# Mamba-2 scan and switch routing: one last routing group of eight units, two experts limited after 16 units, and the first job read and turned like the others

## The chip, the cores and the metric

The kernel runs on one core of a Trainium2 chip. The metric is the device time of one execution in microseconds (us). Of nine runs of the kernel before, the median is 258.06 us, the lowest 257.04 and the highest 258.99.

## The reference, cut to what matters

Two blocks follow each other. The first is a state-space scan: for 4 batches, 8 heads and 768 positions, each head keeps a 16 x 32 state that fades with `a`, and the output is `C` times the state. The reference does it in chunks; the kernel takes chunks of 128 positions, with the same result. The second block sends each of the 3072 tokens (256 wide) to one of eight experts, the one with the largest logit, and multiplies what the expert gives by the softmax weight of that expert.

```python
M = einsum('bhin,bhjn->bhij', Cc, Bc) * L          # masked, decayed scores
y[:, :, sl] = einsum('bhij,bhjd->bhid', M, xc) + y_inter
state = decay_full * state + sum(Bx, axis=2)
...
x = y.transpose(0, 2, 1, 3).reshape(N, 256)
logits = x @ w_gate
expert_idx = argmax(logits, axis=1)
for e in range(8):
    mask = expert_idx == e
    out[mask] = gate_w[mask, None] * (maximum(x[mask] @ w1[e], 0) @ w2[e])
```

## The kernel before

**Units and steps.** A unit is one batch and one chunk of 128 positions, all eight heads: 24 units. A step `d` takes two units, 2d and 2d + 1, and there are 12 steps (`ND`), written out in an order made by hand (L756 to L848; no planner moves instructions, each engine runs its own in the order in which they are emitted). In a step:

- `scores` (L270) multiplies C by B on TensorE; it is emitted at the end of the step before. `weigh` (L276) masks the result on VectorE into the tile M.
- `y_old` (L315) adds what the carried state gives, `y_own` (L325) what the chunk itself gives, both into the PSUM tile `y_ps`.
- `own` (L282) makes the chunk's own part of the new state, in columns 256 to 383 of the first bank of `y_ps` (`A_ps`). `state` (L301) takes it out on ScalarE, `faded` and `whole` add the old state. In the last two steps there is none of this.
- `turned` (L333) copies `y_ps` to the SBUF tile yT on ScalarE. One step later `rows(k)`, k = d - 1 (L341), multiplies yT by a constant on TensorE, which gives token rows and their partial logits in the PSUM tile `r_ps`. `rows_out` (L347) scales them into a row tile on VectorE, and `logits_of` (L364) sums the logits.

**Routing.** Units are routed in groups (`RGS`, L27), six of four units. When a group's rows are there, `choose` (L369) and `count` (L404) find each token's expert and count them; one step later `rank` (L379, TensorE) and `ranked` (L395, VectorE) give each token its place in the DRAM tensor `x_hbm`, in which each expert has an area of its own. `place` (L417) sends a unit's 128 rows there with an indirect DMA of GpSimd; these wait in a list `todo`. An expert's first 256 rows are its first job, the rest its second. So that a first job can be loaded before all tokens are routed, `cut` (L425) raises the expert's count to at least 256 after a group: later tokens then go to the second job. Expert 0 is limited after 16 units (step 9), expert 1 after 20 (step 11). Rows of a first job that no token got were emptied at the start.

**Jobs.** After the loop, the scan's tiles are given back (`att.close()`, L849), and PSUM is divided anew: four banks `h_ps` and two `y_ps` (L539). Jobs 0 to 7 are the experts' first 256 rows. `m_load` (L468) reads a job's rows from `x_hbm`, on the DMA queue of SyncE (SP), behind the places of all rows written before it. For jobs from 1 on it reads them as xb, in four DMAs, such that VectorE's 32 x 32 block transpose (`m_xT`, L521) gives the transposed xT, and once more the rows' ends as lt. Job 0 reads whole rows (tile xs, one DMA), and `m_xT0` (L511) turns them with four TensorE transposes and two ScalarE copies. `gates` (L494) works out the softmax weight on VectorE with one exponential on ScalarE. `m_h` (L560) makes the up products, eight blocks f of 128, with a relu each on ScalarE; `between(f)` (L868) hangs other work between the blocks. `m_y` (L587) makes the down products, `put` (L574) scales them and sends them out with an indirect DMA of GpSimd. The second jobs go in pairs (L619), with a size chosen at run time from the counts: 128 to 192 rows in steps of four.

After the loop, the order before is: the places still in `todo` (units 16 to 19), four weight loads, `m_load(1)`, then rows, rows_out and logits of step 11, `m_xT0`, `choose` and `count` of the last group (units 20 to 23), `gates` of job 0, and the jobs. The last group's rank, its four places and the loads of jobs 2 and 3, with eight weight loads between them, hang behind block 1 of job 0. `over` (L436), behind block 4 of job 1, checks the counts and finds the pairs' sizes.

Of the kernel before, what the change touches and what calls it, by code (L numbers as in the profile page):

```python
# [13 lines left out]
ALU = mybir.AluOpType  # L14
# [11 lines left out]
AMIN = 0.75  # L26
RGS = [4, 4, 4, 4, 4, 4]  # L27
CUT = 4
# [19 lines left out]
def ssd_then_moe(ctx, tc, xs_in, ae_in, wgx, w_gate, w1, w2, gx, gb, gc, ga, out):  # L48
# [232 lines left out]

    def own(d):  # L282
        if d // NP == NC - 1:
            return
        for s in range(2):
            for q in range(4):
                nc.tensor.matmul(A_ps[32 * q:32 * q + 32, 64 * s:64 * s + 64],
                                 lhsT=st[2 * d + s]["B"][:, 32 * q:32 * q + 32],
                                 rhs=st[2 * d + s]["xp"][:, 64 * q:64 * q + 64], start=(s == 0), stop=True,
                                 skip_group_check=True)  # L290
# [41 lines left out]

    def turned(d, a=0, b=KT):  # L333
        if a == 0:
            sd[d]["yT"] = wk.tile([128, KT, 2 * CH], FP32, name="yT")
        nc.scalar.copy(out=sd[d]["yT"][:, a:b], in_=y_ps[:, a:b, 0:2 * CH])  # L336

    rt = [(sm if i < CUT else sm2).tile([128, n, W], FP32, name=f"rows{i}") for i, n in enumerate(RGS)]
    grp = [g for g, n in enumerate(RGS) for _ in range(n)]

    def rows(d):  # L341
        for t, s in [(t, s) for t in range(KT) for s in range(2)]:
            nc.tensor.matmul(r_ps[:, s, 256 * t:256 * t + 160], lhsT=sd[d]["yT"][:, t, CH * s:CH * s + CH],  # L343
                                 rhs=turn[:, t].rearrange("p e h -> p (e h)"), start=True, stop=True,
                                 skip_group_check=True)

    def rows_out(d):  # L347
        n = 2 * d
        g = grp[n]
        k = n - R0[g]  # L350
        for a, b, o in ((0, D, 0), (D, DE, DM)):
            nc.vector.tensor_tensor(
                out=rt[g][:, k:k + 2, o:o + KT * 4 * (b - a)].rearrange("p s (t e h) -> p s t e h", t=KT, h=4),
                in0=r_ps.rearrange("p s (t z) -> p s t z", t=KT)[:, :, :, 4 * a:4 * b].rearrange(
                    "p s t (e h) -> p s t e h", h=4),
                in1=bc(Er[:, n:n + 2].rearrange("p s (t h) -> p s t h", h=4)[:, :, :, None, :],
                       [128, 2, KT, b - a, 4]), op=ALU.mult)
# [62 lines left out]
    def counts(g):  # L420
        p = r_ps[:, 1, 460:460 + E]
        nc.tensor.matmul(p, lhsT=ones_bf, rhs=cnt[:, g], start=True, stop=True, skip_group_check=True)
        return p

    def cut(e):  # L425


        p = r_ps[:, 1, 460:460 + E]
        c = cnt[0:1, CUT + e, e:e + 1]
        nc.vector.tensor_scalar(out=less[:, e:e + 1], in0=p[0:1, e:e + 1], scalar1=-float(P1), scalar2=0.0, op0=ALU.add,  # L430
                                op1=ALU.min)
        nc.vector.tensor_tensor(out=c, in0=c, in1=less[:, e:e + 1], op=ALU.subtract)
        if e == 0:
            nc.vector.tensor_reduce(bad[:, 0:1], p[0:1, 0:2], axis=AX, op=ALU.min)

    def over():  # L436
        p = r_ps[:, 1, 460:460 + E + 1]
        nc.tensor.matmul(p[:, 0:E], lhsT=ones_bf, rhs=cnt[:, len(RGS)], start=True, stop=True, skip_group_check=True)
# [29 lines left out]
    def m_load(i):  # L468


        p, e = jobs[i]
        if i == 0:
            xs = mo.tile([128, 2, W], FP32, name="xs")
            nc.sync.dma_start(out=xs, in_=x_hbm[e * NR:e * NR + P1, :].rearrange("(t p) w -> p t w", p=128))
            ex[i]["xs"] = xs
            ex[i]["lt"] = xs[:, :, DM:W]
            return
        r0, n = e * NR + P1 * p, (P1, P2)[p]
        xb = mo.tile([128, P1 // 32 * 64], FP32, name="xb", bufs=4)
        for c in range(4):  # L480
            nc.sync.dma_start(out=xb[32 * c:32 * c + 32, 0:2 * n].rearrange("p (r z) -> p r z", z=64),
                              in_=x_hbm[r0:r0 + n, 64 * c:64 * c + 64].rearrange("(r j) z -> j r z", j=32))
        ex[i]["xb"] = xb[:, 0:2 * n].rearrange("p (r i k) -> p k r i", k=KT, i=32)
        lt = mo.tile([128, 2, MID], FP32, name="lt", bufs=7)[:, 0:2 - p]
        nc.sync.dma_start(out=lt, in_=x_hbm[r0:r0 + 128 * (2 - p), DM:W].rearrange("(t p) w -> p t w", p=128))
        ex[i]["lt"] = lt
        if p and e % 2 == 0:
            lh = mo.tile([128, 1, MID], FP32, name="lh", bufs=3)
            for u in range(2):
                q = r0 + u * NR + 128  # L490
                nc.sync.dma_start(out=lh[64 * u:64 * u + 64, 0], in_=x_hbm[q:q + 64, DM:W])
            ex[i]["lh"] = ex[i + 1]["lh"] = lh
# [17 lines left out]

    def m_xT0():  # L511

        ex[0]["xT"] = mo.tile([128, KT, P1], FP32, name="xT", bufs=4)
        for k in range(KT):
            q = h_next()[:, 0:P1]
            for t in range(2):
                xs = ex[0]["xs"][:, t, 0:DM].rearrange("p (i k) -> p i k", k=KT)
                nc.tensor.transpose(q[:, 128 * t:128 * t + 128], xs[:, :, k], ident)
            nc.scalar.copy(ex[0]["xT"][:, k], q)  # L519

    def m_xT(i):  # L521
        p, e = jobs[i]
        n = (P1, P2)[p]
        for j in range(i, i + 1 + p):
            ex[j]["xT"] = mo.tile([128, KT, P1], FP32, name="xT", bufs=4)
            nc.vector.transpose(ex[j]["xT"][:, :, 0:n].rearrange("p k (r j) -> p k r j", j=32), ex[j]["xb"])  # L526
        for j in range(i, i + 1 + p):
            ex[j]["g"] = gates(ex[j]["lt"], 2 - p)
        if p:
            ex[i]["gh"] = gates(ex[i]["lh"], 1)  # L530

    H, Y, turn_no = [], [], [0, 0]
    hT_all = [mo.tile([128, FT, P1], FP32, name=f"hT{k}") for k in range(3)]
# [5 lines left out]
    def psum(pp):  # L539
        for k in range(4):  # L540
            H.append(pp.tile([128, 512], FP32, name=f"h_ps{k}"))
        for k in range(2):
            Y.append(pp.tile([128, 512], FP32, name=f"y_ps{k}"))

# [173 lines left out]
    with tc.manual_schedule():  # L718
# [37 lines left out]
        for d in range(ND):  # L756
# [23 lines left out]
            if k >= 0:  # L780
                rows(k)
            own(d)
            if d == 0 or d == 4:
# [4 lines left out]
            q = late.get(d)  # L788
            e_cut = {9: 0, 11: 1}.get(d)
            if q is not None:  # L790
                rank(q)
                if e_cut is not None:
                    counts(CUT + e_cut)
            weigh(2 * d)
            weigh(2 * d + 1)
            if d == 0:
                take_totals(0)
                inverse(0, p0, 4, 12)
            if d < ND - 1:
                for s in range(2):  # L800
                    y_own(d, s, range(NH))
                if d == 4:
                    turn_both(1)
                turned(d)
                if d == 4:
                    take_both(1)
            else:
                for t in range(KT):
                    for s in range(2):
                        y_own(d, s, range(4 * t, 4 * t + 4))  # L810
                for t in range(KT):
                    turned(d, t, t + 1)
            state(d)
# [3 lines left out]
            if q is not None:  # L817
                ranked(q)
                if e_cut is not None:
                    cut(e_cut)  # L820
                todo += list(range(R0[q], R0[q] + RGS[q]))
            if k >= 0:
                rows_out(k)
                if d == 4:
                    take_totals(1)
            if d == 0:
                route_consts()
            if k >= 0:
                logits_of(k)
# [15 lines left out]
            if d == 10:  # L845
                m_load(0)
            if d == 11:
                weakest()  # L848
        att.close()  # L849
        w2pool = ctx.enter_context(tc.tile_pool(name="w2pool", bufs=1, reuse_waits="tile"))  # L850
        pp = ctx.enter_context(tc.tile_pool(name="pp", bufs=1, space=PSUM, reuse_waits="tile"))
        psum(pp)
        for e in range(EW, E):
            w_sb.append([w2pool.tile([128, KT * F], FP32, name=f"w{u + 1}_{e}") for u in range(2)])
        while todo:
            place(todo.pop(0))
        for k in range(4):
            load_w(1, 1, k)
        m_load(1)
        rows(ND - 1)  # L860
        rows_out(ND - 1)
        logits_of(ND - 1)
        m_xT0()
        choose(LAST)
        count(LAST)
        ex[0]["g"] = gates(ex[0]["lt"], 2)
        for i in range(E):
            def between(f):  # L868
                if i == 0:
                    if f == 1:  # L870
                        rank(LAST)
# [3 lines left out]
                        m_load(2)  # L875
                        for k in range(8):
                            load_w(2, *divmod(k, 4))
                        m_load(3)
# [104 lines left out]
```

## Time and profile before

| | |
|---|---|
| median of 9 runs | 258.06 us |
| the profiled execution | 257.07 us |
| its span, first to last instruction | 255.3 us |
| mean granted TensorE clock | 0.983 |
| busy: TensorE | 242.0 us (95%) |
| busy: VectorE, ScalarE, GpSimd | 88.3, 88.9, 84.4 us (33 to 35%) |
| up products of the experts (L557) | 512 matmuls, 91.1 us |
| down products (L592) | 384 matmuls, 85.1 us |
| DMA | 39.75 MB, mean 156 GB/s |

The timeline has one row for instructions of one form that follow each other on an engine: start and length in us, engine, line, operation, tiles, shapes, count, and in brackets the idle time before it and what ended that. "PE" is TensorE, "DVE" VectorE, "ACT" ScalarE, "POOL" GpSimd, "SPq" the DMA issues of SyncE. In the table of windows a row has the stretch, its length, the busy time and count of each engine, the granted TensorE clock as a share, the DMA share and GB/s. L12 is line 12 of the kernel before. A wait's releaser is inferred from semaphore events; ends of matmuls are modelled.

### The profile page before, as it was taken

The numbers are of one execution on the slowest core, as the hardware profiler recorded it, in microseconds if no ns is written. First come the engines' busy times: TensorE is split into PE (matmuls) and PEld (weight loads), VectorE is DVE, ScalarE is ACT, GpSimd is POOL, SyncE is SP. The second block draws the span as 40 slices with busy tenths as digits, with TensorE's granted clock in tenths as the row PEclk, the third lists the DMA queues.
The fourth block names the chain that finished last, engine by engine and source line by source line (L and its number), as shares of the span: only waits on it lengthen the run. The fifth ranks groups of instructions, "written<-read, shape, count | busy, mean of one in ns | idle before, by whom it ended". The sixth has DMA issues, their size and how long they took to land. (4 is left out here: it accounts for less than half of the span.)

```text
span 255.3 us, 5488 instructions
## 1 busy us (share of the span) xinstructions
PE 242.0 (95%) x2020; PEld 203.4 (80%) x2020; DVE 88.3 (35%) x278; ACT 88.9 (35%) x291; POOL 84.4 (33%) x149
## 2 busy tenths in 40 slices
PE   7899899879699999999999999999999999999992
PEld 4677677656488888888888888888998968989781
DVE  5899787657551051020201020303305104221000
ACT  4575657540133222314051423323150520524300
POOL 3655778863606303251423211030310201313031
PEclk9999999997989999999999999999999999999998
DMA  6999978425432599696867779452121200101001
GB/s 177 338 353 329 340 232 272 178 83 181 150 84 108 150 297 290 209 255 206 234 233 200 268 180 289 79 121 43 32 55 34 57 5 16 45 8 38 3 15 44
DMA packets 35319, 39.75 MB, mean 156 GB/s; under 512 B 20604, under 2 KB 22718, under 8 KB 35264
## 3 DMA queue, kind: packets, MB, share of 16 engines
q1 hardware_dynamic: 32272, 30.37, 41.1%
q0 software_dynamic: 2880, 8.66, 9.0%
q8 instruction: 27, 0.44, 0.7%
q14 instruction: 28, 0.23, 0.3%
q10 hardware_dynamic: 112, 0.05, 0.1%
HBM read 29.72 MB, written 9.86 MB: 155 GB/s over the span
## 5 line engine op out<-in xcount | busy, mean ns | idle before, releaser
L557 PE MATMUL h_ps<-xT,w 128*128 128x256 f32 (+3 forms) x512 | 91.1, 337 | 0.3 <-ACT xT L519 0.2
L557 PEld LDWEIGHTS h_ps<-xT,w 128*128 128x128 f32 x512 | 81.6, 192 | 8.2 <-DVE t_gt L508 0.7
L592 PE MATMUL y_ps<-w,hT 128*128 128x256 f32 x384 | 85.1, 380 | 0.0
L592 PEld LDWEIGHTS y_ps<-w,hT 128*128 128x128 f32 x384 | 72.6, 190 | 10.5 <-issue 0.8
L570 POOL DMA_INDIRECT out_dram<-yo,lt x22 | 21.8, 989 | 62.0 <-DVE yo L577 31.4
L566 ACT ACTIVATE hT<-h_ps 128x256 f32<-128x256 f32 x64 | 24.0, 382 | 26.2 <-PE h_ps L557 20.5
L505 DVE TENSOR_REDUCE t_se<-t_sub 128x1 f32<-128x8 f32 (+1 forms) x20 | 3.3, 165 | 85.6 <-ACT t_sub L503 83.0
L278 DVE TENSOR_TENSOR M<-g,mask 128x1024 f32<-128x1024 f32 x24 | 28.3, 1219 | 8.4 <-PE g L273 5.8
L412 POOL DMA_INDIRECT x_hbm<-rows,pos x24 | 23.8, 990 | 16.4 <-DVE less L430 5.8
L632 ACT ACTIVATE hT<-h_ps 128x128 f32<-128x128 f32 (+2 forms) x64 | 18.0, 291 | 23.7 <-PE h_ps L557 23.1
L579 ACT ACTIVATE yo<-y_ps,t_gt 128x256 f32<-128x256 f32 x14 | 6.6, 473 | 41.1 <-PE y_ps L592 41.1
L343 PEld LDWEIGHTS r<-turn,yT 128*128 128x128 f32 x96 | 13.5, 192 | 7.7 <-issue 4.3
L412 POOL DMA_INDIRECT x_hbm<-zrows,rest x8 | 7.7, 961 | 35.8 <-DMA lt<-x_hbm 23.3
L343 PE MATMUL r<-turn,yT 128*128 128x160 f32 x96 | 16.4, 314 | 3.2 <-issue 3.0
L330 PE MATMUL y<-M,xp 128*32 128x128 f32 x384 | 15.5, 282 | 3.3 <-DVE M L278 2.5
L336 ACT COPY yT<-y 128x512 f32<-128x512 f32 (+1 forms) x13 | 7.1, 553 | 28.9 <-PE y L330 20.6
L526 DVE STREAM_TRANSPOSE xT<-xb 128x384 f32<-128x384 f32 (+1 forms) x15 | 9.2, 630 | 20.1 <-DMA xb<-x_hbm 20.0
L261 ACT ACTIVATE cm<-xs_n,par 128x128 f32<-128x128 f32 x46 | 15.0, 417 | 1.8 <-DMA xs_n<-in_xs_dram 1.8
L266 POOL TENSOR_TENSOR xp<-xs_n,Ei 128x256 f32<-128x256 f32 x23 | 13.7, 617 | 5.3 <-DVE xp L266 3.3
L330 PEld LDWEIGHTS y<-M,xp 128*32 128x32 f32 x384 | 10.5, 111 | 6.2 <-issue 4.3
L273 PE MATMUL g<-cm,xs_n 32*128 32x256 f32 x192 | 15.2, 423 | 0.0
L570 POOL DMA_INDIRECT out_dram<-yh,lh x4 | 3.9, 983 | 32.7 <-ACT yh L606 21.0
(122 smaller groups left out, 146.0 us busy)
## 6 DMA issues: line engine op xcount, KB each, us to landing
w<-in_w_dram SPq DMA_DIRECT2D x64, 256.0 KB
xs_n<-in_xs_dram SPq DMA_DIRECT2D x20, 320.0 KB
xb<-x_hbm SPq DMA_DIRECT2D x28, 64.0 KB
xb<-x_hbm SPq DMA_DIRECT2D x32, 48.0 KB
xs_n<-in_xs_dram SPq DMA_DIRECT2D x4, 192.0 KB
x_hbm<-zrows SPq DMA_DIRECT2D x1, 672.0 KB
lt<-x_hbm SPq DMA_DIRECT2D x7, 80.0 KB
xs_n<-in_xs_dram SPq DMA_DIRECT2D x4, 128.0 KB
```

Source lines behind the costliest of these rows:

```text
L261: nc.scalar.mul(t[:, u], st[n]["CT"], par[:, u:u + 1])
L266: eng.tensor_tensor(out=t, in0=st[n]["x"].rearrange("p (h d) -> p h d", d=D), in1=bc(Ei[:, n, :, None], [128, NH, D]), op=ALU.mult)
L273: nc.tensor.matmul(g_ps[:, q, n % 2], lhsT=st[n]["BT"][r], rhs=st[n]["cm"][r].rearrange("p u i -> p (u i)"), start=True, stop=True)
L278: nc.vector.tensor_tensor(out=t, in0=g_ps[:, :, n % 2].rearrange("p q (u i) -> p q u i", u=2), in1=bc(mask[:, None, None, :], [128, 4, 2, ...
L330: nc.tensor.matmul(y_ps[o:o + D, h // 4, CH * s:CH * s + CH], lhsT=st[n]["xp"][:, D * h:D * h + D], rhs=st[n]["M"][:, h], start=first, sto ...
L343: nc.tensor.matmul(r_ps[:, s, 256 * t:256 * t + 160], lhsT=sd[d]["yT"][:, t, CH * s:CH * s + CH], rhs=turn[:, t].rearrange("p e h -> p (e ...
L412: s_ = nc.gpsimd.indirect_dma_start(out=x_hbm[:, :], out_offset=bass.IndirectOffsetOnAxis(ap=at, axis=0), in_=row, in_offset=None)
L557: nc.tensor.matmul(p[:, 0:n], lhsT=w[:, c:c + 128], rhs=xT[:, t, 0:n], start=(t == 0), stop=(t == KT - 1))
L566: nc.scalar.activation(ex[i]["hT"][:, f, 0:n], q, func=ACT.Relu)
L570: return nc.gpsimd.indirect_dma_start(out=out[:, :], out_offset=bass.IndirectOffsetOnAxis(ap=tok, axis=0), in_=yo[:, :], in_offset=None, b ...
L592: nc.tensor.matmul(p, lhsT=ex[i]["hT"][:, f, 128 * t:128 * t + 128], rhs=w_sb[e][1][:, f * DM:f * DM + DM], start=(f == 0), stop=(f == FT ...
L632: nc.scalar.activation(ex[i + u]["hT"][:, f, 0:n], q, func=ACT.Relu)
```

## The change

- `RGS` becomes [4, 4, 4, 4, 8]: units 16 to 23 are one group, routed after the loop. Its rank hangs behind block 4 of job 0, with eight places and the loads of jobs 2 and 3.
- `cut` limits experts 0 and 1 together, at step 9. The counts' place in `r_ps` moves by 32 columns.
- Job 0 is read and turned as the others are; both `m_load(0)` and `m_load(1)` are emitted at step 10. `gates` of jobs 0 to 7 moves from `m_xT` to block 1 of the job itself.
- `rows(10)` moves from the head of step 11 to behind its own outputs, and its rows_out and logits behind that. `rows(11)` writes to the new `y_ps` tile, one tile of two banks, in place of `r_ps`. The own outputs of step 11 go in the order of the other steps, and are copied at once, not in halves.
- `own` moves behind `y_old` and the rank from step 2 on; its first matmul then does not start a new sum, since that of `y_old` in the same bank does.
- The eight loads of expert 2's weights move from block 1 of job 0 to right behind the loop, and `weakest` from step 11 to step 9.

```diff
-RGS = [4, 4, 4, 4, 4, 4]
+RGS = [4, 4, 4, 4, 8]
...
     def own(d):
...
-                                 rhs=st[2 * d + s]["xp"][:, 64 * q:64 * q + 64], start=(s == 0), stop=True,
+                                 rhs=st[2 * d + s]["xp"][:, 64 * q:64 * q + 64], start=(s == 0 and d < NP), stop=True,
...
-    def turned(d, a=0, b=KT):
-        if a == 0:
-            sd[d]["yT"] = wk.tile([128, KT, 2 * CH], FP32, name="yT")
-        nc.scalar.copy(out=sd[d]["yT"][:, a:b], in_=y_ps[:, a:b, 0:2 * CH])
+    def turned(d):
+        sd[d]["yT"] = wk.tile([128, KT, 2 * CH], FP32, name="yT")
+        nc.scalar.copy(out=sd[d]["yT"], in_=y_ps[:, :, 0:2 * CH])
...
-    def rows(d):
+    def rows(d, to=r_ps):
...
-    def rows_out(d):
+    def rows_out(d, of=r_ps):
...
     def counts(g):
-        p = r_ps[:, 1, 460:460 + E]
+        p = r_ps[:, 1, 492:492 + E]
...
-    def cut(e):
+    def cut():
-        p = r_ps[:, 1, 460:460 + E]
-        c = cnt[0:1, CUT + e, e:e + 1]
-        nc.vector.tensor_scalar(out=less[:, e:e + 1], in0=p[0:1, e:e + 1], scalar1=-float(P1), scalar2=0.0, op0=ALU.add,
-                                op1=ALU.min)
-        nc.vector.tensor_tensor(out=c, in0=c, in1=less[:, e:e + 1], op=ALU.subtract)
-        if e == 0:
-            nc.vector.tensor_reduce(bad[:, 0:1], p[0:1, 0:2], axis=AX, op=ALU.min)
+        p = r_ps[:, 1, 492:492 + E]
+        c = cnt[0:1, CUT, 0:2]
+        nc.vector.tensor_scalar(out=less, in0=p[0:1, 0:2], scalar1=-float(P1), scalar2=0.0, op0=ALU.add, op1=ALU.min)
+        nc.vector.tensor_tensor(out=c, in0=c, in1=less, op=ALU.subtract)
+        nc.vector.tensor_reduce(bad[:, 0:1], p[0:1, 0:2], axis=AX, op=ALU.min)
...
     def m_load(i):
-        if i == 0:
-            xs = mo.tile([128, 2, W], FP32, name="xs")
-            nc.sync.dma_start(out=xs, in_=x_hbm[e * NR:e * NR + P1, :].rearrange("(t p) w -> p t w", p=128))
...
-            return
...
-    def m_xT0():
-        ex[0]["xT"] = mo.tile([128, KT, P1], FP32, name="xT", bufs=4)
-        for k in range(KT):
-            q = h_next()[:, 0:P1]
-            for t in range(2):
-                xs = ex[0]["xs"][:, t, 0:DM].rearrange("p (i k) -> p i k", k=KT)
-                nc.tensor.transpose(q[:, 128 * t:128 * t + 128], xs[:, :, k], ident)
-            nc.scalar.copy(ex[0]["xT"][:, k], q)
...
     def m_xT(i):
...
-        for j in range(i, i + 1 + p):
-            ex[j]["g"] = gates(ex[j]["lt"], 2 - p)
         if p:
+            for j in range(i, i + 2):
+                ex[j]["g"] = gates(ex[j]["lt"], 1)
             ex[i]["gh"] = gates(ex[i]["lh"], 1)
...
     def psum(pp):
...
+        Y_all.append(pp.tile([128, 2, 512], FP32, name="y_ps"))
         for k in range(2):
-            Y.append(pp.tile([128, 512], FP32, name=f"y_ps{k}"))
+            Y.append(Y_all[0][:, k])
...
             if k >= 0:
-                rows(k)
-            own(d)
+                if d < ND - 1:
+                    rows(k)
+            if d < NP:
+                own(d)
...
             y_old(d)
             q = late.get(d)
-            e_cut = {9: 0, 11: 1}.get(d)
             if q is not None:
                 rank(q)
-                if e_cut is not None:
-                    counts(CUT + e_cut)
+                if q == CUT - 1:
+                    counts(CUT)
+            if d >= NP:
+                own(d)
             weigh(2 * d)
             weigh(2 * d + 1)
...
-            if k >= 0:
+            if k >= 0 and d < ND - 1:
                 rows_out(k)
...
             if d == 10:
                 m_load(0)
-            if d == 11:
+                m_load(1)
+            if d == 9:
                 weakest()
+        rows(ND - 2)
         att.close()
...
         psum(pp)
...
-        while todo:
-            place(todo.pop(0))
-        for k in range(4):
-            load_w(1, 1, k)
-        m_load(1)
-        rows(ND - 1)
-        rows_out(ND - 1)
+        for e, u in ((1, 1), (2, 0), (2, 1)):
+            for k in range(4):
+                load_w(e, u, k)
+        rows(ND - 1, Y_all[0])
+        rows_out(ND - 2)
+        logits_of(ND - 2)
+        m_xT(0)
+        rows_out(ND - 1, Y_all[0])
         logits_of(ND - 1)
-        m_xT0()
         choose(LAST)
         count(LAST)
-        ex[0]["g"] = gates(ex[0]["lt"], 2)
         for i in range(E):
             def between(f):
+                if f == 1:
+                    ex[i]["g"] = gates(ex[i]["lt"], 2)
                 if i == 0:
-                    if f == 1:
+                    if f == FT // 2:
                         rank(LAST)
                         ranked(LAST)
                         for k in range(R0[LAST], NU):
                             place(k)
                         m_load(2)
-                        for k in range(8):
-                            load_w(2, *divmod(k, 4))
                         m_load(3)
                     return
```

## The prediction

> **What bounds the kernel now.** I read the page first. TensorE is busy for 95% of the span, and the timeline shows it working without a hole from 78.8 us to the end: one expert's up and down products take 6.9 us each, 13.8 us per expert. An edit can therefore gain only by letting that run begin earlier, or lose by making a later job's rows late. So I looked at how the run begins. The windows around the change of stages (PE, PEld, DVE, ACT and POOL busy, then the granted clock):
>
> ```profile
> 58.00:60.00 2.00, 1.87 (x32) 1.10 (x32) 1.97 (x4) 0.00 (x0) 1.38 (x3) 0.77 0.24 90
> 60.00:62.00 2.00, 2.00 (x20) 1.22 (x16) 0.61 (x4) 0.58 (x1) 0.23 (x2) 0.50 0.72 214
> ...
> 66.00:68.00 2.00, 0.11 (x1) 0.11 (x2) 0.91 (x4) 0.53 (x2) 1.56 (x5) 1.00 0.22 86
> 68.00:70.00 2.00, 1.92 (x12) 1.52 (x12) 0.72 (x2) 0.45 (x3) 1.78 (x3) 0.83 0.45 172
> 70.00:72.00 2.00, 1.92 (x5) 1.56 (x6) 1.58 (x8) 0.51 (x3) 0.36 (x3) 0.50 0.23 86
> 72.00:74.00 2.00, 2.00 (x13) 1.47 (x12) 0.72 (x5) 0.80 (x3) 0.00 (x0) 0.82 0.38 74
> ```
>
> TensorE is nearly idle from 66 to 68 us, and then runs at half clock from about 69 to 73 us; a first such pair lies at 56 to 62 us. The timeline gives the instructions:
>
> ```profile
> 56.56 2.36 DVE L278 TENSOR_TENSOR M<-g,mask 128x1024 f32<-128x1024 f32 x2 [2.39 <-PE r L343]
> ...
> 62.23 2.36 DVE L278 TENSOR_TENSOR M<-g,mask 128x1024 f32<-128x1024 f32 x2 [1.51 <-PE g L273]
> ...
> 64.51 1.08 PE L330 MATMUL y<-M,xp 128*32 128x128 f32 x32
> ...
> 67.47 0.65 ACT L336 COPY yT<-y 128x256 f32<-128x256 f32 x2 [6.63 <-remote]
> ...
> 67.89 1.35 PE L343 MATMUL r<-turn,yT 128*128 128x160 f32 x8 [2.30 <-issue]
> ...
> 69.08 0.83 PE L518 MATMUL h_ps<-ident,xs 128*128 128x128 f32 x4
> ...
> 69.66 0.66 ACT L519 COPY xT<-h_ps 128x256 f32<-128x256 f32 x2 [1.55 <-PE h_ps L518]
> ...
> 70.08 3.29 PE L557 MATMUL h_ps<-xT,w 128*128 128x256 f32 x8 [0.17 <-ACT xT L519]
> ```
>
> The last own outputs (L330) end at 65.59 by their row, yet ScalarE's copy of them starts only at 67.47, 1.88 us later; everything behind it is one chain up to the first up product at 70.08. That product and the rank beside it run until the first down product at about 78.61: 8.53 us, where a warm one takes 6.9 us.
>
> **The order at step 11.** Masking ends at 62.23 + 2.36 = 64.59, so the second unit's own outputs cannot end before 64.59 + half of 1.08 = about 65.2. Taking rows(10) (1.54 us at 62.09), the rank and count of units 16 to 19 (0.4 us at 64.15) and their DVE instructions away in front gains nothing: all of it lay beside the masking. Behind 65.2 the new chain is: rows(10), 1.35 us, to 66.55; on VectorE rows_out, 0.88, logits, 0.29, and the transpose that replaces TensorE's, 0.71 (row of L526), with some 0.15 of gaps: 68.6; the first up product at 68.7. The copy of step 11 (0.58) and rows(11) (1.35) lie beside this, and the new PSUM tile lets rows(11) start before rows_out(10) has read the old one. Four TensorE transposes (0.83) and two ScalarE copies (0.66) go. Against 70.08 that is **1.4 us earlier**. This takes the own outputs to be released when their row ends. Why they were not is not shown; GpSimd was issuing places back to back from 65.33 to 70.13, as it was from 52.95 to 57.76 around the other late release (M at 56.56, 2.39 us late). In the new kernel no places are left at step 11, so I take the second late release as gone and the first as unchanged: the order up to step 10 is nearly the same.
>
> **The clock.** With rows of two steps back to back and the up product at 68.7, TensorE idles 0.8 us there in place of 2.3, and I take the half clock at 69 to 73 us as gone. The up product then takes 6.9 us, and the last group's rank has ten small products in place of six: 0.24 us becomes 0.4. Together 7.3 us against 8.53: **1.2 us less**. The first down product starts at 68.7 + 7.3 = 76.0 in place of 78.6, **2.6 us earlier**. If the clock still falls, 1.2 of the 2.6 is lost.
>
> The Trainium skill, "TensorE: Matmul & The Clock Gate", section "What's actually happening", says that the clock is halved after at least one idle window of about 3.4 us. The rows show half clock behind gaps of 1.8 us (56.1 to 57.9) and 2.3 us; a rule of 3.4 us of idleness would have had neither. By that rule filling a 2.3 us gap buys no clock, and the gain would be 1.4 us alone; I go by the rows.
>
> **The first jobs' rows.** m_load(0) was one DMA at 59.49; now both first jobs take four xb and one lt each, 1.81 + 0.45 us of issue (rows at 71.82 and 73.68), so job 0's end at 61.8 and job 1's at 64.1 on SP. Job 1's in the trace landed 3.8 us after its first issue (transpose at 75.61). Job 0's rows are there at about 63.4, and VectorE wants them at 67.8: 4.4 us of cover. Behind them SP issues twelve weight loads of 0.55 us, done by 71; the second expert's down weights are wanted at 90, the third's at 97. That experts 0 and 1 are both limited after 16 units costs no instruction: the three VectorE ones of step 9 stay, those of step 11 go. Counted from the reference's inputs, 246 and 222 of these units' tokens choose them, so 34 later tokens of expert 1 move into its second job: 377 in all in place of 343, and expert 0 has 382 in both kernels. Both need 256 + 128, so the pair's size stays. Cost nothing.
>
> **The last group.** rank now stands at the fifth up product of job 0: 68.7 + 4.3 = 73.0, ranked to 73.9 (0.2 us each). Eight places at 1.27 us (0.96 + memset and gap) end at 84.1. The trace's last place starts 2.64 us before m_load(2) is issued (80.71, 83.35), so m_load(2) goes at about 85.4, its rows land at 89.2, and m_xT(2) ends at 90. Job 2 begins at 76.0 + 6.9 + 13.8 + 0.1 = 96.8: 6.8 us of cover. Were that gone, each us would be one on the end. In the trace the first of these places waited until 76.89, by the memory order behind m_load(1)'s read; that read is now early. put's sends queue behind eight places in place of four; yo has three buffers, and the third is wanted at 93.
>
> **Own state and gates.** own (L287, 0.43 us at 50.67) goes behind y_old from step 2. TensorE waited for its inputs 1.9 us in all (xp 1.4, S 0.5), so y_old could cover up to that; but y_own waits for masking anyway. Bounds: 1.9 us gained, 0.43 lost in each of eight steps were it to push y_own back; I take 0, since the 0.43 us stands ahead of y_own either way. gates move from the preceding job to f = 1: seven VectorE instructions of about 0.2 us and one exponential. VectorE idles for some 10 us in each such job, so 0; if lt were late, ScalarE's relus would queue behind the exponential and four h_ps banks would cover 3.4 us.
>
> **The sum.** -1.4 - 1.2 = -2.6 us on the profiled execution's 257.07 (span 255.3, 1.8 around it): 254.5. The median, 258.06, is 1.0 above that execution; the same step gives **255.4 us**.
>
> **Rivals.** (a) The late release of the own outputs stays, 1.88 us, because places had nothing to do with it, and the clock stays up: the own outputs are free at 67.1, the up product starts at 67.1 + 3.5 = 70.6, 0.5 later than now, and 1.2 comes back from the clock: 257.4. For it speaks that the page names no releaser there but "remote"; against it, that the ordinary copies follow their L330 row within 0.5 us. The Trainium skill, "Perfetto Trace Analysis", section "Tensor Engine Instruction (MATMUL, LD_WEIGHTS)", says that a matmul's end is estimated, so the row's 65.59 may be too early; no row decides it.
>
> (b) **Slower:** the chain behind the own outputs is longer than before: 3.5 us (rows 1.35, three VectorE instructions, gaps) against 70.08 - 67.47 = 2.6 from copy to up product. It decides if the late release stays and the clock falls again: +0.5 +0.2 (rank), with up to 0.6 more if rows(10) also runs at half clock: 258.9 (258.7 to 259.4).
>
> (c) The first late release (2.39 us at step 10) and its half clock go too, since own and the masking instructions around it move: 2.4 more, and up to 1.7 from the clock (58 to 62.5 us): 252.3. For it: own stands between the rank and the masking of step 9. Against: the places at 52.95 are the same.
>
> (d) The change does not do what it says: the early start is given back, when twelve weight loads (3.1 MB) beside the places make job 2's rows late by more than 6.8 us: about 258. DMA share was 0.21 to 0.53 from 74 to 90 us, which speaks against it.
>
> **Chances.** Forecast 0.48 (254.3 to 256.4 alone), (a) 0.20, (b) 0.15, (c) 0.12, (d) 0.05. The range 252.4 to 258.2 holds the forecast, (a), half of (c) and half of (d). A measurement can tell 0.3%, 0.8 us, from no change. Faster than 257.3: forecast, (c) and half of (a), 0.70; within 0.3%: half of (a) and (d), 0.15; slower than 258.8: (b), 0.15.
>
> **What would show it.** Right: first up product at 68 to 69.5, PEclk 1.0 from 66 to 76, the step-11 copy within 0.3 us of its L330 row's end, first down product near 76, and job 2's transpose before its up product by over 3 us. Wrong: a "remote" wait of the copy of over 1.5 us; a clock of 0.5 in any window of 64 to 76; a PE wait for xT or a DMA at 90 to 100. A first half clock missing at 58 to 62 means (c).

## The result, and the profile after

The changed kernel takes **280.45 us** (median of 10 runs, 279.14 to 282.72). The kernel before took 257.69 us beside it (median of 31 runs). The ratio is 1.0927, interval [1.0890, 1.0964]: 9% slower, where 1% faster was forecast, and far outside the range. The profiled execution took 282.99 us, with a span of 281.2 us in place of 255.3. Ratios here and below are formed from undisturbed runs alone, so that they are not always the quotient of two medians.

The page after. The line of the down products gives busy time and mean, and behind the bar the idle time just ahead of them and what ended most of it; PEclk is the granted clock in 40 slices of 7.0 us:

```profile
PEclk9999999975999999999999999999979988989999
...
L574 PE MATMUL y_ps<-w,hT 128*128 128x256 f32 x384 | 93.3, 398 | 16.0 <-DVE yo L559 9.5
```

The same line of the page before:

```profile
L592 PE MATMUL y_ps<-w,hT 128*128 128x256 f32 x384 | 85.1, 380 | 0.0
```

The down products had no idle time ahead of them before (85.1 us busy, 380 ns each, 0.0 idle). Now 16.0 us of waiting stand ahead of them, and they are busy for 8.2 us more. Together that is 24.2 of the 25.9 us by which the span grew; the other 1.7 us are as long as a new wait of job 1's up products for a relu (1.66 us, ended at 91.74; the same wait is looked at under e5). The dip of the clock near the tenth slice is the old one, longer; the dips in the last third are new.

What TensorE waits for, in all: us in total, times, longest.

```profile
PE y_ps L574 <- DVE yo L559: 9.5, 5, 2.9
PE y_ps L574 <- ACT yo L561: 4.0, 7, 0.6
...
PE y_ps L574 <- ACT yh L581: 1.3, 2, 0.7
PE y_ps L574 <- ACT yh L588: 1.2, 2, 0.6
```

All four are the same wait: a down product waits for `yo` or `yh`, which is the scaling that `put` does on the result of *other* down products. 9.5 + 4.0 + 1.3 + 1.2 = 16.0 us, all the idle time that the page gives. Before, no line of this list named `yo` or `yh`.

The timeline shows how one such wait comes about, in an ordinary job and then in a pair of second jobs:

```profile
95.44 3.62 PE L574 MATMUL y_ps<-w,hT 128*128 128x256 f32 x16
...
99.09 0.47 ACT L561 ACTIVATE yo<-y_ps,t_gt 128x256 f32<-128x256 f32 x1 [3.07 <-PE y_ps L574]
...
99.62 3.72 PE L574 MATMUL y_ps<-w,hT 128*128 128x256 f32 x16 [0.56 <-ACT yo L561]
...
204.98 0.16 DVE L499 RECIPROCAL t_gt<-t_se 128x1 f32<-128x1 f32 x1
205.09 0.48 DVE L559 TENSOR_SCALAR yo<-y_ps,t_gt 128x256 f32<-128x256 f32 x1
...
205.63 5.41 PE L574 MATMUL y_ps<-w,hT 128*128 128x256 f32 x16 [2.87 <-DVE yo L559]
```

A job's 32 down products are two groups of 16, one for each bank of `y_ps`. The first group ends at 95.44 + 3.62 = 99.06. Before, the second followed at once (7.07 us for 32, in one line). Now it starts at 99.62, when ScalarE has scaled the first group's bank, although it writes the other bank. In the pairs it is worse: `put` of the first bank stands on VectorE behind the small instructions of the pair's `gates` (three calls, six instructions each), so the second group waits 2.87 us. That gap also costs clock, by the windows of the same stretch (busy time of PE, PEld, DVE, ACT and POOL with their counts, then PEclk, DMA share, GB/s):

```profile
204.00:206.00 2.00, 0.37 (x2) 0.34 (x3) 1.14 (x6) 0.21 (x1) 0.00 (x0) 1.00 0.55 98
206.00:208.00 2.00, 2.00 (x7) 1.61 (x6) 0.00 (x0) 0.00 (x0) 0.98 (x1) 0.55 0.12 36
208.00:210.00 2.00, 2.00 (x7) 1.60 (x6) 0.00 (x0) 0.00 (x0) 0.00 (x0) 0.60 0.13 42
```

TensorE runs at about half clock for 3.4 us behind the gap, and the 16 products take 5.41 us in place of 3.72. The same is seen behind the waits of 2.66 us (ended at 230.50) and 2.72 us (ended at 249.94). Three times 1.5 to 1.7 us is about 5 of the 8.2 us by which the down products are longer; I put the rest, some 3 us over 24 groups, down to each group's own start and end, which no longer overlap.

**The stretch that the prediction was about**, 55 to 79 us, first by windows of 5 us and then by instructions:

```profile
55.00:60.00 5.00, 1.31 (x33) 0.83 (x32) 2.45 (x3) 0.53 (x2) 3.61 (x6) 0.94 0.28 105
60.00:65.00 5.00, 4.57 (x57) 3.05 (x61) 2.76 (x5) 0.59 (x1) 0.00 (x0) 0.50 0.57 110
65.00:70.00 5.00, 4.95 (x44) 4.14 (x35) 1.30 (x3) 0.59 (x1) 0.00 (x0) 0.53 0.84 239
```

```profile
57.55 2.36 DVE L278 TENSOR_TENSOR M<-g,mask 128x1024 f32<-128x1024 f32 x2 [3.35 <-issue]
...
64.59 2.21 PE L331 MATMUL y<-M,xp 128*32 128x128 f32 x32 [0.38 <-DVE M L278]
...
66.92 0.59 ACT L336 COPY yT<-y 128x512 f32<-128x512 f32 x1 [5.09 <-PE y L331]
...
71.16 4.58 PE L539 MATMUL h_ps<-xT,w 128*128 128x256 f32 x20 [0.57 <-DVE xT L507]
...
78.73 1.46 PE L574 MATMUL y_ps<-w,hT 128*128 128x256 f32 x6
```

The second late release is gone, as forecast: the own outputs end at 66.80 and their copy starts 0.12 us later (1.88 before). But the first one is longer: masking of step 10 starts at 57.55 (56.56 before, behind 2.39 us of idle time; here 3.35). Behind it one stretch of half clock reaches from about 59.4 to 69.7 us, where there had been two of 3.4 us each with a warm stretch between. The first up product starts at 71.16 (70.08 before, 68.7 forecast) and the first down product at 78.73 (78.83 before, 76.0 forecast). So the early part of the change gained nothing in this execution, and everything behind it lost 26 us.

### The profile page after: what moved, and what is told of

Read it like the earlier page. It is cut to its first block, busy times and chain, and to the rows that moved or that the text cites. A ratio compares the mean times of both kernels' runs of the same rounds, so it can differ in the third digit from the quotient of the medians.

```text
span 281.2 us, 5469 instructions
## 1 busy us (share of the span) xinstructions
PE 249.4 (89%) x2013; PEld 205.8 (73%) x2013; DVE 88.0 (31%) x272; ACT 88.4 (31%) x288; POOL 84.3 (30%) x147
## 5 line engine op out<-in xcount | busy, mean ns | idle before, releaser
L574 PE MATMUL y_ps<-w,hT 128*128 128x256 f32 x384 | 93.3, 398 | 16.0 <-DVE yo L559 9.5
L574 PEld LDWEIGHTS y_ps<-w,hT 128*128 128x128 f32 x384 | 75.0, 199 | 32.6 <-DVE yo L559 11.5
L539 PE MATMUL h_ps<-xT,w 128*128 128x256 f32 (+3 forms) x512 | 89.9, 334 | 2.2 <-ACT hT L548 1.7
L539 PEld LDWEIGHTS h_ps<-xT,w 128*128 128x128 f32 x512 | 80.7, 190 | 9.5 <-ACT hT L548 2.1
L552 POOL DMA_INDIRECT out_dram<-yo,lt x24 | 23.8, 990 | 104.5 <-ACT yo L561 53.4
L614 ACT ACTIVATE hT<-h_ps 128x128 f32<-128x128 f32 (+2 forms) x64 | 18.7, 292 | 39.9 <-PE h_ps L539 39.7
L331 PE MATMUL y<-M,xp 128*32 128x128 f32 x384 | 16.6, 293 | 5.6 <-POOL xp L266 3.3
L559 DVE TENSOR_SCALAR yo<-y_ps,t_gt 128x256 f32<-128x256 f32 x10 | 4.8, 484 | 42.2 <-PE y_ps L574 42.2
L331 PEld LDWEIGHTS y<-M,xp 128*32 128x32 f32 x384 | 11.2, 116 | 8.7 <-issue 3.6
L336 ACT COPY yT<-y 128x512 f32<-128x512 f32 x12 | 7.0, 586 | 28.2 <-PE y L331 23.2
```

The costliest lines, as they stand in the source:

```text
L331: nc.tensor.matmul(y_ps[o:o + D, h // 4, CH * s:CH * s + CH], lhsT=st[n]["xp"][:, D * h:D * h + D], rhs=st[n]["M"][:, h], start=first, sto ...
L539: nc.tensor.matmul(p[:, 0:n], lhsT=w[:, c:c + 128], rhs=xT[:, t, 0:n], start=(t == 0), stop=(t == KT - 1))
L552: return nc.gpsimd.indirect_dma_start(out=out[:, :], out_offset=bass.IndirectOffsetOnAxis(ap=tok, axis=0), in_=yo[:, :], in_offset=None, b ...
L574: nc.tensor.matmul(p, lhsT=ex[i]["hT"][:, f, 128 * t:128 * t + 128], rhs=w_sb[e][1][:, f * DM:f * DM + DM], start=(f == 0), stop=(f == FT ...
L614: nc.scalar.activation(ex[i + u]["hT"][:, f, 0:n], q, func=ACT.Relu)
```

## The experiments

Theories: **(A)** `y_ps` as one tile of two banks makes each down group wait for the scaling of the other bank. **(B)** `gates` at f = 1 keep ScalarE and VectorE from `put`. **(C)** the late release at step 10 sets the time. For what is left without A: **(P)** results of TensorE reach the other engines late while GpSimd issues indirect DMAs closely one behind the other; **(Q)** the lateness has nothing to do with them.

### e1: the change with two PSUM tiles

```diff
-        Y_all.append(pp.tile([128, 2, 512], FP32, name="y_ps"))
         for k in range(2):
-            Y.append(Y_all[0][:, k])
+            Y.append(pp.tile([128, 512], FP32, name=f"y_ps{k}"))
+        Y_all.append(Y)
```

`rows` of step 11 writes each tile by itself, and `rows_out` reads them with four VectorE instructions in place of two.

> The changed kernel with y_ps as two tiles of one bank, as before; rows of step 11 go into the two, and their scaling takes four VectorE instructions in place of two. Theory A (the down products wait, since y_ps is one tile: a group of down products may not begin before the group in the other bank has been scaled): TensorE's waits on yo and yh (16.0 us) go, and with them the refills behind each and the half clocks between 205 and 255 us; 256 to 259 us. Theory B (the gates, now behind block 1 of the same job, hold ScalarE's relus): the waits on yo stay or turn into waits on hT; 276 us or more. Theory C (the late release at step 10 and its half clock, 59 to 70 us): 276 us or more, for the first down product began at the same time as before.

Measured: 257.62 us (12 runs), ratio 1.0059 [1.0012, 1.0106]. The page's line of the down products:

```profile
L584 PE MATMUL y_ps<-w,hT 128*128 128x256 f32 x384 | 85.1, 380 | 0.0
```

No waiting, and 85.1 us as before. This edit alone takes 23 us off. A holds; B and C, whose parts are all still in this kernel, do not carry the loss.

### e2: the kernel before with one PSUM tile

```diff
+        y_all = pp.tile([128, 2, 512], FP32, name="y_ps")
         for k in range(2):
-            Y.append(pp.tile([128, 512], FP32, name=f"y_ps{k}"))
+            Y.append(y_all[:, k])
```

> The kernel before with only y_ps made one tile of two banks, nothing else of the change. Theory A: 277 to 283 us, with waits of TensorE on yo and yh of about 16 us in all. Theory B and C: within 1 us of before.

Measured: 279.29 us (4 runs, 276.39 to 281.04; the traced one 277.80), against 257.0 of the kernel before beside it. The waits of TensorE are those of the changed kernel:

```profile
PE y_ps L593 <- DVE yo L578: 9.4, 5, 2.9
...
PE y_ps L593 <- ACT yo L580: 2.8, 5, 0.6
PE y_ps L593 <- ACT yh L600: 1.3, 2, 0.7
PE y_ps L593 <- ACT yh L607: 1.2, 2, 0.6
```

The same two lines, put alone into the old kernel, cost 21 to 22 us. The cause is settled from both sides.

### e3: the change with the gates where they were

```diff
-                if f == 1:
-                    ex[i]["g"] = gates(ex[i]["lt"], 2)
```

and the calls of before in `m_xT` and ahead of the jobs.

> The changed kernel, one y_ps tile kept, with the gates of jobs 1 to 7 back behind the transposes of the job before and those of job 0 ahead of the jobs. Theory A: within 2 us of the changed kernel (280). Theory B: back to 260 or less.

Measured: 280.12 us, ratio 1.0947 [1.0867, 1.1027]. No difference from the changed kernel's 1.0927: moving the gates cost and gained nothing, as the prediction had it, and B is out.

### e4: e1 with the four places of units 12 to 15 moved

With A repaired, what is left is 0.6% slower than before and not 1% faster. Here the places that GpSimd issues around 52 to 57 us go behind `whole` and `scaled_x` of step 10.

```diff
-            while todo and d == 10:
-                place(todo.pop(0))
-            if todo:
+            if todo and d < 10:
...
+            while todo and d == 10:
+                place(todo.pop(0))
             faded(d)
...
-            if d == 9:
-                for _ in range(2):
-                    place(todo.pop(0))
```

> As e1, and the four places of units 12 to 15 (two at the end of step 9, two at the head of step 10) all moved behind whole and scaled_x of step 10, so GpSimd issues none while the masking of step 10 waits. If places issued back to back cause the late release (theory P), the masking of step 10 starts at about 54 in place of 56.6 to 57.6, the half clock at 59 goes or shortens, and the kernel is 1.5 to 4 us faster than e1, though job 0's rows are asked for some 3 us later. If they do not (theory Q), the masking is as late as before and the kernel is within 1 us of e1, or slower by up to 1 if job 0's rows come late.

Measured: 259.68 us, ratio 1.0124 [1.0065, 1.0184]. Masking of step 10 in e1, and then in e4:

```profile
58.20 2.36 DVE L278 TENSOR_TENSOR M<-g,mask 128x1024 f32<-128x1024 f32 x2 [3.99 <-remote]
```

```profile
55.34 2.34 DVE L278 TENSOR_TENSOR M<-g,mask 128x1024 f32<-128x1024 f32 x2
...
70.69 4.58 PE L549 MATMUL h_ps<-xT,w 128*128 128x256 f32 x20 [0.84 <-DVE xT L517]
```

The 3.99 us of waiting at step 10 is gone with the places, 2.9 us earlier. But the masking of step 11 is late in its place (63.14), next to where the places now are, and job 1 is held longer (job 2 starts at 103.45, in e1 at 100.03). So the lateness moves with the places, which speaks for P; but the time got worse, by 2.1 us against e1, which neither theory had said.

### e5 and e6: places further apart

A memset of 128 x 512 on GpSimd (0.54 us) stands ahead of a place: in e5 ahead of the last eight (units 16 to 23), in e6 ahead of those of units 12 to 15 too. All else is e1.

```diff
-            nc.gpsimd.memset(spare, 0.0)
+            nc.gpsimd.memset(pace if slow else spare, 0.0)
```

> As e1, with the one-element memset in front of each of the eight places of the last group made a memset of 128 x 512 (some 0.5 us by the memset of 128 x 336, 0.38), so that the places stand further apart; the rows of job 2 come some 4 us later. Theory P (TensorE's completions reach the others late while GpSimd issues indirect DMAs closely): job 1's up products take about 7.0 us in place of 8.7, the wait of TensorE on hT (1.5 us) goes, and the kernel is 1 to 2 us faster than e1. Theory Q (the wait on hT has another cause, the gates in that job or the loads): within 0.7 us of e1.

> As e5, and the four places of units 12 to 15 at steps 9 and 10 paced too. Theory P: the masking of step 10 starts 2 us or more earlier than in e1 (58.2), the half clock at 60 us goes, and the kernel is 2 to 4 us faster than e5 (252 to 254). Theory Q: the masking is as late as in e1, and the time that of e5.

Measured for e5: 256.27 us, ratio 0.9955 [0.9916, 0.9994]. What it acts on is job 1. In e1 the timeline of TensorE and ScalarE has:

```profile
84.40 4.48 PE L549 MATMUL h_ps<-xT,w 128*128 128x256 f32 x20
...
87.15 0.38 ACT L558 ACTIVATE hT<-h_ps 128x256 f32<-128x256 f32 x1 [1.68 <-PE h_ps L549]
90.00 0.38 ACT L558 ACTIVATE hT<-h_ps 128x256 f32<-128x256 f32 x1 [2.46 <-PE r L447]
...
90.38 0.92 ACT L558 ACTIVATE hT<-h_ps 128x256 f32<-128x256 f32 x3
90.43 2.86 PE L549 MATMUL h_ps<-xT,w 128*128 128x256 f32 x12 [1.52 <-ACT hT L558]
93.13 7.07 PE L584 MATMUL y_ps<-w,hT 128*128 128x256 f32 x32
```

Twenty up products run from 84.40 to 88.88, four for each of ScalarE's relus; yet one relu starts at 87.15, the next at 90.00, and then three at once. TensorE runs out of free banks and waits 1.52 us. GpSimd was issuing eight places and two sends back to back until 88.2. The up part of job 1 takes 93.13 - 84.40 = 8.73 us, where the kernel before took 92.78 - 85.73 = 7.05. In e5:

```profile
85.02 4.48 PE L550 MATMUL h_ps<-xT,w 128*128 128x256 f32 x20
...
92.06 7.07 PE L585 MATMUL y_ps<-w,hT 128*128 128x256 f32 x32
```

7.04 us, and the wait for hT is gone. Masking of step 10, whose places are as they were, is still late (58.91, behind 4.15 us).

Measured for e6: **253.69 us**, ratio 0.9859 [0.9821, 0.9898]. Places of GpSimd in e1 and then in e6 (start, duration):

```profile
53.80 0.96 POOL L422 DMA_INDIRECT x_hbm<-rows,pos  x1 [0.21 <-issue]
54.76 0.09 POOL L421 MEMSET spare<- 1x1 f32 x1
55.07 0.96 POOL L422 DMA_INDIRECT x_hbm<-rows,pos  x1 [0.22 <-issue]
```

```profile
53.93 0.54 POOL L422 MEMSET pace<- 128x512 f32 x1
54.64 0.97 POOL L423 DMA_INDIRECT x_hbm<-rows,pos  x1 [0.17 <-issue]
55.61 0.54 POOL L422 MEMSET pace<- 128x512 f32 x1
56.31 0.97 POOL L423 DMA_INDIRECT x_hbm<-rows,pos  x1 [0.17 <-issue]
```

They start 1.67 us apart in place of 1.27. Other engines in e6:

```profile
54.55 2.34 DVE L279 TENSOR_TENSOR M<-g,mask 128x1024 f32<-128x1024 f32 x2
...
65.67 4.58 PE L550 MATMUL h_ps<-xT,w 128*128 128x256 f32 x20 [0.87 <-DVE xT L518]
...
73.23 7.07 PE L585 MATMUL y_ps<-w,hT 128*128 128x256 f32 x32
```

Masking of step 10 no longer waits (54.55 against 58.20 in e1), the clock stays up at 60 to 64 us (1.00, against 0.50 and 0.73 in e1), and the first up and down products are 4.3 us earlier than in e1. GpSimd does more work (89.8 us busy against 84.1) and the kernel is faster. That is what P expects and Q does not.

### e7, e10, e16: the kernel before with places further apart

The same memset in the kernel before, for units 12 to 15 alone (e7, and e16 again) and for units 12 to 23 (e10).

> The kernel before with only the four places of units 12 to 15 paced in the same way. Theory P: the masking of step 10, at 56.6 in its trace, starts at 54 to 55, and the kernel is 0.5 to 3 us faster than before, less where job 0's rows, asked for some 2 us later, hold its start. Theory Q: within 0.7 us of before.

> The kernel before with all twelve places of units 12 to 23 paced, not only those of units 12 to 15. Theory P: the copy of step 11 is not released late; but the places of units 16 to 19 end some 2 us later, and with them job 1's and job 2's rows, which in e7 already held job 2 by 1.7 us: 252 to 256 us, not faster than e6.

> e7 (before with the four places of units 12 to 15 paced) once more. Theory P with sessions: 2 to 4 us faster than before where before shows late releases, within 1.5 us of it or slower where it does not.

Measured: e7 253.69 us, ratio 0.9893 [0.9842, 0.9945]; e16 254.27 us, ratio 0.9979 [0.9938, 1.0020]; e10 255.07 us, ratio 1.0160 [1.0103, 1.0217]. In e7 the first up product comes at 65.76 (70.08 before), but job 1 is then held:

```profile
90.87 5.01 PE L593 MATMUL y_ps<-w,hT 128*128 128x256 f32 x22 [1.39 <-ACT hT L567]
```

The down products of job 1 wait 1.39 us for a relu; in e16 2.15 and in e10 2.6 us, with a stretch of half clock behind it in both (92.7 to 96.1 us in e16). The traces show what holds the relu. In e16:

```profile
89.51 0.71 DVE L527 STREAM_TRANSPOSE xT<-xb 128x512 f32<-128x512 f32 x1 [2.77 <-DMA xb<-x_hbm]
...
91.13 0.21 ACT L504 ACTIVATE t_sub<-t_sub 128x16 f32<-128x16 f32 x1 [6.07 <-DVE t_sub L503]
91.25 0.92 ACT L567 ACTIVATE hT<-h_ps 128x256 f32<-128x256 f32 x3
```

In the kernel before, the `gates` of job 2 are emitted in job 1, so their exponential (t_sub) stands ahead of job 1's last relus on ScalarE, and it waits for job 2's rows. These are no earlier although TensorE is: VectorE's transpose waits 2.07 us for their DMA in e7, 2.77 in e16 and 3.14 in e10. This is not the lateness that P speaks of, and it stays in e10, where all places are spread. The change has moved `gates` to the job itself, and e6 has no such wait; e6 with the gates at their old place was not tried. So job 2's up products start at 95.73 in e7 and at 98.21 in e16, where two jobs at full speed behind the first up product would have them at about 94.1. The early start is kept only as far as job 1 is not held. In the comparison that has both, e7 and e6 share one median (253.69 us); in the other, e16 is 2.2 us behind e6's repetition e15. The old order gains less surely from the same edit than the new order, and pacing the later places too (e10) only lost.

### e8: the change with two tiles and six routing groups

```diff
-RGS = [4, 4, 4, 4, 8]
+RGS = [4, 4, 4, 4, 4, 4]
...
+        while todo:
+            place(todo.pop(0))
         for e, u in ((1, 1), (2, 0), (2, 1)):
```

> As e1, with six groups of four units again: units 16 to 19 are ranked at step 11 and placed right behind the loop, units 20 to 23 in job 0. Theory P: the own outputs of step 11 or rows behind them are released late again, first up product 0.5 us or more later than in e1, but job 1 has no wait on hT; in sum within 1.5 us of e1. If the group of eight as such is what costs against before, it is 1 to 2 us faster than e1.

Measured: 255.74 us, ratio 0.9949 [0.9914, 0.9984]. The first up product is at 70.53 (69.93 in e1), and no up product of job 1 waits for hT; its down products start at 91.92 (93.13 in e1). By the two ratios (taken beside different runs of the kernel before) the single last group of eight, with its eight places in a row, is a loss of about 1% as the change has it: it gains 0.6 us at the start and loses more in job 1.

### e9, e11, e12: how much distance, and by what

On e6: a memset of 128 x 192 (e9), a copy of 128 x 256 on GpSimd in place of the memset (e11), a memset of 128 x 1024 for units 12 to 15 (e12).

> As e6, with the pacing memset at 128 x 192 in place of 128 x 512 (some 0.25 us in place of 0.54; places 1.4 us apart in place of 1.68, and 1.27 in e1). Theory P: between e1 and e6, 254 to 257 us, with the masking of step 10 between 54.6 and 58.2. If the gain comes from something else that the tile pace does (its place in SBUF, another instruction order), the time is that of e6.

> As e6, but the pacing instruction is a GpSimd copy of 128 x 256 from SBUF to SBUF (some 0.5 us) in place of the memset. Theory P needs only time between the places: within 1 us of e6 (253.7). If it is the memset as such, the time goes back to that of e1.

> As e6, with a memset of 128 x 1024 (some 1.05 us) in front of the four places of units 12 to 15. Theory P: nothing more to gain at step 10, as no half clock is left there; whole and scaled_x of step 10 and job 0's rows come 2 us later: 253.5 to 256 us.

Measured: e9 250.25 us, ratio 0.9972 [0.9927, 1.0017]; e11 251.10 us, 1.0024 [0.9978, 1.0071]; e12 252.15 us, 1.0057 [1.0026, 1.0087]. These runs, with e10, were made beside a kernel before that took 251.52 us (29 runs), 5 to 6 us less than in every other comparison, on the same chip that had given 257.54 earlier. In absolute time e9 and e11 are no slower than e6; in ratio nothing is gained. No trace of that faster kernel before was taken, so whether its late releases were missing is not known. Two things on record show that it was not the places alone: e9, e11 and e12 do the same as e6 up to the first spread place, yet masking of step 9 starts at 46.98 to 47.90 there (49.95 in e6, 50.12 in e15); and the granted clock of that kernel before is 0.997 in the mean, against 0.990 beside e6.

Masking of step 10 starts at 52.20 in e9 and 53.40 in e11, without a wait in either, but then job 0's rows are late: the first up product comes at 64.30 behind 2.31 us and at 65.98 behind 2.78 us of waiting for xT, and VectorE's transpose had waited for the DMA of xb. So neither the right distance nor memset against copy is decided by these runs. In e12 masking of step 10 is early (51.93), but the first up product is later (67.13) and the clock falls at 58 to 65 us: more distance is not better. GpSimd is then late for its own work in the scan: y_old of step 11 waits 3.64 us, to 59.78, for `whole` (tile S), which stands behind the places.

### e13, e14, e15: the kernel before, e1 and e6 again

No new edits: the kernel before against itself, and the two kernels on which the account rests, on another chip. "P with sessions" means that the late releases are there in some comparisons and missing in others.

> The kernel before, unchanged, for a trace of it in the same session as e14 to e16. Theory P with sessions: where its median is near 257 the trace shows the masking of step 10 over 1.5 us behind its scores and the copy of step 11 over 1 us behind the own outputs; where it is near 251 it shows neither. Theory Q: the late releases are there at either time.

> e1 once more, beside before. Theory P with sessions: in a session without late releases e1 gains what was forecast, 1 to 3 us against before; in one with them it is within 1.5 us of before again.

> e6 once more. Theory P with sessions: 2 to 5 us faster than before where before shows late releases; within 1 us of e1, or slower by up to 1.5 us, where it does not. Theory Q: the same distance to e1 in either session.

Measured: e13 257.34 us, ratio 0.9982 [0.9912, 1.0051], which shows what "no change" looks like (its trace, of an execution of 259.52 us, has both late releases: masking of step 10 behind 4.53 us, the copy of step 11 1.1 us behind its row's end); e14 257.57 us, 1.0051 [1.0013, 1.0089], as e1; e15 **252.12 us**, 0.9860 [0.9808, 0.9912], as e6. Masking of step 10 starts at 57.74 in e14, behind 4.03 us of idle time, and at 54.71 in e15, behind none. The 251.5 us of the comparison above did not come back, so "P with sessions" was not put to its test.

## Why the prediction was wrong

**The step that failed** is an edit costed at nothing. The prediction said of it: "The copy of step 11 (0.58) and rows(11) (1.35) lie beside this, and the new PSUM tile lets rows(11) start before rows_out(10) has read the old one." It looked at what the new tile lets happen ahead of the jobs, and not at who uses it afterwards. All 24 groups of 16 down products go through that tile, and what had been two tiles, each waited for by itself, was now one: a write into either bank waits for the last read of both. The rows would have priced it: a scaling takes 0.47 to 0.48 us, and sixteen times (eight jobs, and two in each of four pairs) a down group now waits for the scaling of the one ahead of it, some 8 us (the waits came to 0.56 to 0.67 us each). In three of these `gates` stand ahead of the scaling on VectorE, with 2.7 to 2.9 us of waiting in place of 0.6, some 6.5 us more, and each then lost 1.5 to 1.7 us to the clock. Measured (e1, e2): 21 to 23 us. None of the rivals contained this.

With this step repaired (e1, e14) the change is still 0.5 to 0.6% slower and not 1% faster. The other steps, each against the profile:

- **The second late release goes**: right, in the change (0.12 us behind the row's end in place of 1.88) and in e1.
- **The first late release "as unchanged"**: mis-sized. Masking of step 10 starts at 58.20 in e1 and 57.74 in e14, against 56.56. So the second unit's own outputs in e1 end at 66.08 + 0.64 = 66.7 and not at 65.2, and the first up product comes at 69.93, only 0.15 us earlier than before and not 1.4. From the own outputs on the chain is as worked out: 3.2 us, against 3.5. What made this release longer was not tried by itself. `own` had moved, but it has in e8 too, where the wait is 2.62 us, near the 2.39 of before.
- **"I take the half clock at 69 to 73 us as gone"**: right in e1 (1.00 from 64 us on; up part and rank 77.49 - 69.93 = 7.56 us, against 7.3 forecast and 8.53 before, where the prediction took 78.61, the first weight load, for the first down product at 78.83), wrong in the changed kernel, where half clock lasted until 69.7. The first down product is thus 1.3 us earlier in e1 in place of the 2.6.
- **The last group's places** were costed by whether job 2's rows are late. They are not: no wait of TensorE for them is in the lists of the changed kernel and e1. But the eight places lie beside job 1's relus, and job 1 lost 8.73 - 7.05 = 1.7 us there, which eats the 1.3 us. The prediction had named places back to back as what stood beside both late releases, and did not ask what the new eight would stand beside.
- **Pair sizes unchanged, first jobs' rows on time, gates and own state at nothing**: the pairs ran with the same sizes (164 and 160 rows beside 128), no wait for these rows in the changed kernel, e1 or e6 (in e9 and e11, with a still earlier scan, there is one); and for the gates e3, with no difference. `gates` is six VectorE instructions, not seven. What the prediction did not see is that their old place holds job 1 once the start is early (e7, e10, e16). The own state was not tried alone.
- **Rival (c)**, the first late release goes too, was put at 252.3 us. e6 and e15 come nearest to that case, made on purpose and with job 1's wait gone too: 253.7 and 252.1 us.

The Trainium skill, "TensorE: Matmul & The Clock Gate", section "What's actually happening", says that the gate looks at free-running windows of about 3.4 us. The stretches of half clock behind the pairs' gaps are 3.4 us long, which agrees; the gaps of 2.66 to 2.87 us ahead of them are shorter than the whole idle window that the same table asks for, as the prediction's rows of 1.8 and 2.3 us were. The length of a gap does not decide by itself either: the wait of 2.78 us in e11 left the clock at 1.00.

**What stays open.** How closely issued indirect DMAs come to hold the other engines is not shown; that the lateness moves with them (e4), goes when they are spread (e5, e6, e15) and comes with eight in a row (e1 against e8) is. Close places do not always do it: four of them 1.27 us apart beside job 0, from 76.89 to 81.67 before and from 76.18 to 80.95 in e8, left the relus beside them at their even 0.86 us. Whether it is the distance or the memset between them is not decided. And why the kernel before once ran at 251.5 us is not known.

The version that beats both kernels is e6, the change with two PSUM tiles and the places 1.67 us apart: ratio 0.986 in both comparisons in which it was run. In the third, its near relatives e9 and e11 gained nothing.

## What to carry to other kernels

Before two buffers are made one, list everybody who uses them later, and price each as if every user waited for all of it: an edit that serves one place ahead of a loop can add a wait to every turn of the loop. A gap in the busiest engine costs twice where the clock falls behind it. Work in a row on an engine that looks idle is not always free; ask what runs beside it, and try it spread. When a start gets earlier, look at what stands in the in-order queues of the helpers: an instruction for a later job, whose data has not come, holds the present one.

## What the runs showed of the hardware

Not expected: while GpSimd issued indirect DMAs 1.27 us apart, VectorE's masking waited 3.99 us (e1) and 4.03 us (e14), beyond the ends of the products that the rows show, and ScalarE's relus came in one burst after a pause of 2.5 us; with the DMAs 1.67 us apart, neither was there. And in the changed kernel's jobs waits of 0.56 us of TensorE left the clock at full, while those of 2.66 to 2.87 us were each followed by some 3.4 us at about half; yet in e9 and e11 waits of 2.31 and 2.78 us were not.
